# Batch 0 of a retention and mixer kernel: queries by head pairs in 1024-byte rows, scores of two units by head halves

## The chip, the cores and the metric

The kernel runs on one core of a Trainium2 chip. The metric is the device time of one execution in microseconds, as the median of several runs. Five engines run their own instruction streams and wait for each other by semaphores: TensorE (PE, with its weight loads shown as PEld), VectorE (DVE), ScalarE (ACT), GpSimd (POOL) and SyncE (SP, which here only issues DMAs).

## What is computed

```
q, k, v: [8, 8, 576, 64] float32           # batch, heads, positions, head size
scores = q @ k.T / 8                       # per batch and head
gamma  = 1 - 2 ** (-5 - head)
Dmat   = gamma ** (i - j) where i >= j, else 0
x      = (scores * Dmat) @ v               # [8, 576, 512], heads side by side
h      = x.T @ U @ V                       # U [576, 32], V [32, 576]: mixing along the positions
u      = x + h.T
out    = u + relu(u @ w1) @ w2             # w1 [512, 2048], w2 [2048, 512]
```

## The kernel before

The decay factorises: gamma^(i-j) = gamma^i * gamma^-j. So values are scaled by gamma^-j (`scale_u`, `scale_v`), the scores are only cut at the diagonal (`mask_u`), and the rows of the result are scaled by gamma^i (`XS_u`). Within a block of positions the scores are computed outright; what comes from earlier blocks goes through a running state k^T v (`ST_u`, copied to bf16 by `Sblk`) that the queries are multiplied with (`QS_u`). The MLP is the bulk of the work: `y1_items` holds the matmuls with w1 and the relu (L513, L518), `y2_items` those with w2 (L547).

The first two batches are handled apart from the rest. Each is cut in two *units* of 256 positions and one block of 64 (the "J" block). Batch 0 is units 0 and 1, batch 1 units 2 and 3. In a unit partition p holds positions 2p and 2p+1 of its 256, so that one DMA row has 2 x 64 values (512 bytes) of a head. `load_u(u, which)` issues on SP two DMAs of 256 KB, heads 0-3 and 4-7, for each of k, q and v asked for; they land in tiles of the `stage` pool (15 buffers). `cast_u` makes bf16 of such a tile (POOL, L613), `T_u` turns a whole tensor of a unit by sixteen transposes into one PSUM tile and copies it to SBUF (L628, then L639 on ScalarE or L641 on VectorE). For queries the copy also puts the even and odd positions back in order, so it writes every second element.

`SC_u(u, hh, ...)` computes the scores of four heads (hh 0: heads 0-3, hh 1: heads 4-7) by sixteen matmuls into a PSUM tile: `ps_sc` or `ps_o`, one buffer each, so the next scores in it wait for the mask that empties it. `mask_u` multiplies with the triangle on VectorE (L664). `RV_u` multiplies with the values.

The order on each engine is the order in the code (`manual_schedule`), and each engine takes its instructions in that order. `startup()` (from L812) holds the order up to the first MLP matmuls: first all loads on SP, then casts, turns, scores, masks and scalings. `warm(n)` issues n matmuls with no use for the result. SP gives each DMA one of eight semaphores in turn, so a DMA waits until the one eight places before it has landed. `load_w1(fb)` issues the DMA of a quarter of w1 (1 MB of float32, written as bf16) on POOL, between POOL's casts and scalings; there are four, and MLP columns f = 0-3, 4-7, ... need one each. `first_stretch()` (from L932) then mixes the MLP of batch 0 (`y(n)` issues the next n columns) with units 2 and 3; in each of these, TensorE turns keys and queries between MLP columns. From `main = ...` (L1073) on a merge of lists sets the order for the other batches.

Of the kernel before, what the change touches and what calls it, by code (L numbers as in the profile page):

```python
# [9 lines left out]
FP32 = mybir.dt.float32  # L10
BF16 = mybir.dt.bfloat16
# [25 lines left out]
def kernel(  # L37
# [11 lines left out]
    nc = tc.nc  # L49

    B, H, S, D = q.shape
    dm = H * D
    dff = moe_w_ch1.shape[1]
    R = moe_U.shape[1]
    P = 128
    HALF = 64
    NHP = H // 2
# [14 lines left out]
    stage = pool("stage", 15)  # L72
# [103 lines left out]
    def make_v():  # L176
        for c0, n in ((0, 4 * P), (4 * P, HALF)):
            ps = ps_big.tile([P, 4 * P], FP32, tag="big", name="pv")
            nc.tensor.matmul(
                ps[:, 0:n], fan.rearrange("k g r -> k (g r)"), V_b[:, c0:c0 + n],  # L180
                start=True, stop=True)
            nc.scalar.activation(
                out=V4[:, HALF + c0:HALF + c0 + n], in_=ps[:, 0:n], func=AF.Copy)

    def warm(n, pool_=None, tag="pss"):

        ps = (pool_ or ps_s).tile([P, 4, P], FP32, tag=tag, name="pw")
        for _ in range(n):
            nc.tensor.matmul(  # L189
                ps, ident, ident[:, None, :].to_broadcast([P, 4, P]), start=True, stop=True)  # L190
# [396 lines left out]
    def load_u(u, which):  # L587
        b = u // 2
        t0 = 2 * P * (u % 2) + HALF * b
        for j in which:  # L590
            dram = (q, k, v)[j]
            for hh in range(2):
                t = stage.tile([P, H, D], FP32, tag="stage", name="stage_t")
                un[u]["f", j, hh] = t
                nc.sync.dma_start(  # L595
                    out=t.rearrange("p (h j) d -> p h (j d)", j=2),
                    in_=dram[b, 4 * hh:4 * hh + 4, t0:t0 + 2 * P, :].rearrange(
                        "h (p j) d -> p h (j d)", j=2),
                )

    def unit_views(u, j, hh):
        if j not in un[u]:
            un[u][j] = qk_pool.tile([P, 2, dm], BF16, tag="qk", name="qk")
        w = slice(hh * 4 * D, (hh + 1) * 4 * D)
        return (un[u][j][:, :, w].rearrange("p j (h d) -> p h j d", d=D),
                un[u]["f", j, hh].rearrange("p (h j) d -> p h j d", j=2))
# [17 lines left out]
    def T_u(u, j, eng):  # L624
        pst = ps_big.tile([P, 2 * NHP, P], BF16, tag="big", name="pst")
        for jj in range(2):
            for hp in range(NHP):
                nc.tensor.transpose(  # L628
                    pst[:, jj * NHP + hp, :], un[u][j][:, jj, hp * P:(hp + 1) * P], ident)
        t = qkT_pool.tile([P, 2 * NHP, P], BF16, tag="qkT", name="qkT")  # L630
        un[u]["T", j] = t
        o, i_ = t, pst
        if j == 0:

            o = t.rearrange("p a b -> p (a b)").rearrange(
                "p (hp t j) -> p j hp t", hp=NHP, j=2)
            i_ = pst.rearrange("p (j hp) t -> p j hp t", j=2)
        if eng is nc.scalar:
            nc.scalar.activation(out=o, in_=i_, func=AF.Copy)  # L639
        else:  # L640
            eng.tensor_copy(out=o, in_=i_)  # L641

    def qT(u):
        return un[u]["T", 0].rearrange("p a b -> p (a b)").rearrange(
            "p (hp t) -> p hp t", hp=NHP)

    def SC_u(u, hh, pool_, tag):
        psc = pool_.tile([P, 2, NHP, P], FP32, tag=tag, name="psc")
        kT, qt = un[u]["T", 1], qT(u)
        for hp in range(2):  # L650
            for jj in range(2):
                for s in range(2):
                    for hl in range(2):
                        r = slice(hl * HALF, (hl + 1) * HALF)
                        m = slice(s * HALF, (s + 1) * HALF)
                        nc.tensor.matmul(  # L656
                            psc[m, hl, hp * 2 + jj, :], kT[r, jj * NHP + 2 * hh + hp, m],
                            qt[r, 2 * hh + hp, s * P:(s + 1) * P], start=True, stop=True,
                        )
        un[u]["psc", hh] = psc  # L660

# [30 lines left out]
    def QS_u(u, s, slot):  # L692
        for hp in range(NHP):
            nc.tensor.matmul(
                un[u]["po"][:, s, hp * P:(hp + 1) * P],
                qT(u)[:, hp, s * P:(s + 1) * P], sblk[:, slot, hp, :],
                start=False, stop=True, skip_group_check=True,
            )

# [107 lines left out]
    def cast_unit(u):  # L807
        for j in (1, 0):
            for hh in range(2):
                cast_u(u, j, hh, nc.gpsimd)  # L810

    def startup():  # L812
        load_u(0, (1, 0))
        load_v_rows()
        load_u(1, (1, 0))
        load_u(0, (2,))
        load_u(1, (2,))
        load(0, J, (1, 0, 2), seg=0)
        load_u_rows()
        load(0, J, (1, 0, 2), seg=1)  # L820
        load_u(2, (1, 0, 2))
        load_u(3, (1, 0, 2))
        nc.gpsimd.memset(st["x", 0][HI, J, :], 0.0)

        warm(10)
        cast_unit(0)
        T_u(0, 1, nc.vector)
        warm(5)
        nc.scalar.activation(out=V_b, in_=V_f, func=AF.Copy)
        T_u(0, 0, nc.scalar)  # L830
        make_v()
        warm(3)
        SC_u(0, 0, ps_sc, "psc")
        mask_u(0, 0)
        cast_unit(1)
        T_u(1, 1, nc.scalar)
        SC_u(0, 1, ps_o, "po")
        mask_u(0, 1)
        warm(2)
        T_u(1, 0, nc.scalar)  # L840
        scale_u(0, 0, nc.gpsimd)
        load_w1(0)
        scale_u(1, 0, nc.gpsimd)
        scale_u(1, 1, nc.gpsimd)
        cast_qk(0, J, LO, nc.gpsimd, js=(0,))
        scale_v(0, J, LO, nc.gpsimd)
        load_w1(1)
        cast_qk(0, J, HI, nc.gpsimd)
        scale_v(0, J, HI, nc.gpsimd)
        load_w1(2)  # L850
        scale_u(0, 1, nc.vector)
        warm(6)
        SC_u(1, 0, ps_sc, "psc")
        mask_u(1, 0)
        SC_u(1, 1, ps_o, "po")
        mask_u(1, 1)

        accA = pss_tile()
        accB = ps_big.tile([P, NHP, P], FP32, tag="big", name="pss2")
        ST_u(0, LO, accA, True)  # L860
        Sblk(accA, 0)
        ST_u(0, ALL, accB, True)
        Sblk(accB, 1)
        cast_qk(0, J, LO, nc.scalar, js=(1,))
        po_u(0, ps_sc, "psc")
        warm(2, ps_big, "big")
        RV_u(0, 0)
        RV_u(0, 1)
        QS_u(0, 1, 0)
        XS_u(0)  # L870
        warm(1, ps_big, "big")
        ST_u(1, LO, accB, False)
        Sblk(accB, 2)
        warm(1, ps_big, "big")
        RV_u(1, 0)
        RV_u(1, 1)
        T_J(LO, nc.vector)
        ST_u(1, HI, accB, False)
        Sblk(accB, 3)
        SC_J(LO)  # L880
        mask_J(LO)
        QS_u(1, 0, 1)
        QS_u(1, 1, 2)
        XS_u(1)
        make_ue()

        xT = [ps_big.tile([P, dm], FP32, tag="big", name="xT") for _ in range(3)]

        def to_xT(i, ccs):
            for cc in ccs:  # L890
                nc.tensor.matmul(
                    xT[cc][:, i * P:(i + 1) * P],
                    st["x", 0][:, i, cc * P:(cc + 1) * P], ident,
                    start=(i == 0), stop=True, skip_group_check=True,
                )

        for i in range(2):
            to_xT(i, range(3))
        RV_J(LO)
        QS_J(3)  # L900
        XS_J(LO)
        warm(2, ps_sc, "psc")
        xT.append(ps_sc.tile([P, dm], FP32, tag="psc", name="xT"))
        for i in range(2, J):
            to_xT(i, range(3))
        for i in range(J):
            to_xT(i, (3,))
        MA, _, _, _ = mixer_items(0, 0, split=True)
        MA((ps_o, "po"))
        warm(1)  # L910
        for cc in range(NCC):
            g = slice(cc * R, (cc + 1) * R)
            nc.tensor.matmul(
                xT[cc], st["a", 0][g, :], V4[g, HALF:HALF + 4 * P],
                start=False, stop=True, skip_group_check=True,
            )
        warm(1)
        for cc in range(NCC):
            o = st["uT", 0][:, :, cc, :]
            i_ = xT[cc].rearrange("p (s t) -> p s t", t=P)  # L920
            if cc % 2 == 0:
                nc.scalar.activation(out=o, in_=i_, func=AF.Copy)  # L922
            else:
                nc.vector.tensor_copy(out=o, in_=i_)
# [202 lines left out]
```

## Time and profile before

| | |
|---|---|
| median of 3 runs (lowest, highest) | 320.02 us (319.51, 321.42) |
| span of the profiled execution, first to last instruction | 318.7 us |
| the profiled execution's own time | not recorded apart from its span; the median run is 1.3 us longer than the span |
| busy: PE, DVE, ACT, POOL | 98%, 53%, 43%, 28% of the span |
| mean granted clock of TensorE | 1.00 |
| first MLP matmul (L513) | 23.73 us from the start |
| DMA share in 4 to 32 us | 1.0 to 1.3 of the core's 16 engines |

A profile line of the timeline reads: start, duration, engine, line, operation, output tile <- inputs, shape of output <- input, count, and in brackets the idle time of the engine before it with what ended it. The chain of waits lists start, duration and what the end of the program was waiting for at that time. A line of stages reads: from:to, length, then busy time (and number of instructions) of PE, PEld, DVE, ACT, POOL, then granted clock, DMA share, GB/s. A DMA share can pass 1, because packets of one DMA engine overlap.

### The profile page before, as it was taken

The page shows a single profiled execution, that of the slowest core. Times are in us where ns is not written, and L with a number is a line of the kernel's source. Part 1 is how long each engine was busy: PE and PEld are TensorE (multiplying, and loading weights), DVE is VectorE, ACT ScalarE, POOL GpSimd, SP SyncE. Part 2 cuts the span into 40 slices and gives each one's busy share as a digit, 9 for nine tenths or more (in the row PEclk, how much of TensorE's full clock was granted, in tenths as well). Part 3 has the DMA queues.
Part 4 walks back from the last instruction along what each step waited for, and adds up shares of the span by engine and source line. Part 5 has one row for each costly group of instructions (what it writes and reads, how often), then busy time and mean ns, then how long its engine had stood idle before and what let it go on. Part 6 is the DMA issues. An engine that isn't in the chain of part 4 may idle for free.

```text
span 318.7 us, 9166 instructions
## 1 busy us (share of the span) xinstructions
PE 311.4 (98%) x3929; PEld 167.7 (53%) x3929; DVE 169.1 (53%) x354; ACT 136.7 (43%) x293; POOL 90.3 (28%) x138
## 2 busy tenths in 40 slices
PE   8999899999999999999999999999999999999996
PEld 3564554554444444466644444466644444467544
DVE  5571466447995467545684468545674563500012
ACT  2757557772120465038720375048720463057400
POOL 5762933512232423132241423141241300110000
DMA  7999999999999979699994999598994710620022
GB/s 202 258 204 267 232 198 203 191 203 187 237 212 216 260 156 175 137 242 183 176 184 106 262 177 175 142 248 172 163 202 109 189 37 1 135 81 0 2 84 81
DMA packets 151321, 53.30 MB, mean 167 GB/s; under 512 B 131985, under 2 KB 148753, under 8 KB 151281
## 3 DMA queue, kind: packets, MB, share of 16 engines
q1 hardware_dynamic: 144512, 40.40, 70.2%
q0 software_dynamic: 6768, 12.32, 16.2%
q8 instruction: 30, 0.49, 0.7%
q14 instruction: 11, 0.08, 0.1%
HBM read 36.85 MB, written 9.44 MB: 145 GB/s over the span
## 4 chain that ended last, share of the span: by engine, by line
PE 84%; DMA 7%; ACT 3%; DVE 2%; issue 1%; SPq 1%; POOL 1%; ACTq 0%
PE ps_y L513 37%; PE ps_y L547 35%; DMA stage_t<-in_q_dram 5%; DMA qkT<-qk 2%; PE psc L279 2%; PE ph L454 1%; PE po L344 1%; PE ps_y L558 1%; PE po L361 1%; SPq L595 1%; PE psc L290 1%; PE pa L427 1%; ACT qkT L639 1%; PE psc L656 1%; PE pst L628 1%
## 5 line engine op out<-in xcount | busy, mean ns | idle before, releaser
L518 ACT ACTIVATE y<-ps_y 128x384 bf16<-128x384 f32 (+2 forms) x192 | 89.1, 489 | 105.1 <-PE ps_y L513 104.6
L513 PE MATMUL ps_y<-uT,w_sb 128*128 128x512 bf16 (+3 forms) x768 | 132.2, 326 | 0.7 <-ACT uT L922 0.4
L547 PE MATMUL ps_y<-w_sb,y 128*128 128x512 bf16 x560 | 126.3, 379 | 0.0
L513 PEld LDWEIGHTS <-w_sb 128*128 128x128 bf16 x768 | 70.2, 98 | 51.0 <-issue 2.4
L547 PEld LDWEIGHTS <-y 128*128 128x128 bf16 x560 | 52.7, 98 | 61.3
L536 DVE TENSOR_TENSOR o_sb<-ps_y,u 128x512 f32<-128x512 f32 (+2 forms) x38 | 25.2, 663 | 66.3 <-PE ps_y L547 63.9
L303 DVE TENSOR_TENSOR ret<-psc,tri 64x256 bf16<-64x256 f32 x108 | 45.3, 419 | 1.1
L539 POOL DMA_DIRECT2D out_dram<-o_sb x31 | 17.3, 558 | 98.6 <-DVE o_sb L536 95.7
L255 POOL TENSOR_TENSOR vt<-stage_t,vscale 128x512 bf16<-128x512 f32 (+1 forms) x29 | 30.2, 1041 | 52.3 <-DMA stage_t<-in_v_dram 44.6
L325 DVE TENSOR_TENSOR s_f<-psc,s_f 128x256 f32<-128x256 f32 x42 | 17.8, 423 | 26.2 <-PE psc L290 12.9
L460 DVE TENSOR_TENSOR u<-ph,xt 128x1024 bf16<-128x1024 f32 (+3 forms) x24 | 21.8, 951 | 9.3 <-PE ph L454 9.3
L246 ACT ACTIVATE qk<-stage_t 128x512 bf16<-128x512 f32 x27 | 16.9, 626 | 21.1 <-DMA stage_t<-in_q_dram 15.2
L372 DVE TENSOR_TENSOR xt<-po,qscale 128x512 bf16<-128x512 f32 x27 | 18.4, 681 | 1.8 <-PE po L344 1.8
L244 POOL CAST qk<-stage_t 128x512 bf16<-128x512 f32 x20 | 12.3, 614 | 23.6 <-DMA stage_t<-in_k_dram 21.4
L334 ACT ACTIVATE s_sb<-s_f 128x512 bf16<-128x512 f32 (+1 forms) x27 | 15.5, 575 | 3.8 <-DVE s_f L325 3.8
L315 DVE COPY vs<-vt 64x256 bf16<-64x256 bf16 x54 | 14.3, 265 | 1.2
L664 DVE TENSOR_TENSOR ret<-psc,triU 128x1024 bf16<-128x1024 f32 x8 | 9.6, 1222 | 9.2 <-PE psc L656 9.2
L189 PE MATMUL pw<-ident 128*128 128x512 bf16 x34 | 11.5, 461 | 1.4 <-POOL ident masks.py:199 1.4
L613 POOL CAST qk<-stage_t 128x512 bf16<-128x512 f32 x16 | 9.6, 613 | 9.9 <-DMA stage_t<-in_q_dram 5.3
L323 DVE COPY s_f<-psc 128x256 f32<-128x256 f32 x6 | 2.5, 424 | 16.4 <-PE psc L290 11.3
L279 PEld LDWEIGHTS <-qkT 64*64 64x64 bf16 x432 | 5.6, 107 | 9.6 <-issue 8.5
L433 ACT ACTIVATE a_sb<-pa 128x128 bf16<-128x128 f32 x8 | 2.2, 277 | 18.0 <-PE pa L427 18.0
(112 smaller groups left out, 191.4 us busy)
## 6 DMA issues: line engine op xcount, KB each, us to landing
stage_t<-in_k_dram SPq DMA_DIRECT2D x32, 256.0 KB, 4.8
stage_t<-in_q_dram SPq DMA_DIRECT2D x32, 256.0 KB, 5.3
stage_t<-in_v_dram SPq DMA_DIRECT2D x32, 256.0 KB, 5.5
out_dram<-o_sb POOLq DMA_DIRECT2D x31, 256.0 KB, 4.3
w_sb<-in_moe_w_ch_dram POOLq DMA_DIRECT2D x4, 512.0 KB, 8.0
w_sb<-in_moe_w_ch_dram POOLq DMA_DIRECT2D x8, 256.0 KB, 5.8
stage_t<-in_k_dram SPq DMA_DIRECT2D x8, 128.0 KB, 5.1
stage_t<-in_q_dram SPq DMA_DIRECT2D x8, 128.0 KB, 5.5
```

What stands on the lines that cost most here:

```text
L246: nc.scalar.activation(out=t[rows, 0, :], in_=c["f", 0][rows].rearrange("p h d -> p (h d)"), func=AF.Copy)
L255: (eng or nc.gpsimd).tensor_tensor(out=c["v"][rows], in0=c["f", 2][rows], in1=vscale[rows, i, :, None].to_broadcast([n, H, D]), op=ALU.mult,)
L303: nc.vector.tensor_tensor(out=ret[o, n], in0=c["psc"][t, hl, 0:SW].rearrange("p (hp i) -> p hp i", i=D), in1=tri[t, None, t].to_broadcast( ...
L325: nc.vector.tensor_tensor(out=f[:, t, :], in0=inc, in1=f[:, 1 - t, :], op=ALU.add)
L334: nc.scalar.activation(out=ch[pr, i]["s1"][:, w, :], in_=s_f[:, w, :], func=AF.Copy)
L372: nc.vector.tensor_tensor(out=xt[:, i, :].rearrange("p (hp hl d) -> p hl hp d", hl=2, d=D), in0=c["po"][:, :, 0:NHP * D].rearrange("p hl ( ...
L460: nc.vector.tensor_tensor(out=st["u", par][:, i0 - base:i0 - base + n, w].rearrange("p s (c d) -> p c s d", c=2), in0=ph[k][:, :, 0:n, :], ...
L513: nc.tensor.matmul(ps[:, 0:n, :], w1_sb[:, cc, f * P:(f + 1) * P], st["uT", par][:, c0:c0 + n, cc, :], start=(cc == 0), stop=(cc == NCC - 1),)
L518: nc.scalar.activation(out=st["y1", par][:, f, c0 * P:(c0 + n) * P], in_=ps[:, 0:n, :].rearrange("p s t -> p (s t)"), func=AF.Relu)
L536: nc.vector.tensor_tensor(out=o_sb[:, 0:n], in0=ps[:, 0:n], in1=st["u", par][:, c, w], op=ALU.add)
L539: (nc.sync if last else nc.gpsimd).dma_start(out=out_flat[r0:r0 + P, w], in_=o_sb[:, 0:n])
L547: nc.tensor.matmul(ps, st["y1", par][:, f, c * P:(c + 1) * P], w2_sb[:, f, :], start=(f == 0), stop=(f == NF - 1),)
```

## The change

Queries of batch 0 are no longer loaded by unit. `load_q4(hp)` loads two heads for both units at once: partition p holds positions 4p to 4p+3 of 512, a row is 4 x 64 values (1024 bytes), and there are four such loads of 256 KB, in the four places of the four query loads of before. `cast_q4` makes bf16 of one of them, `T_q4(g, engs)` turns two of them (four heads) by eight transposes and copies the result with one instruction per head pair, one on each engine named; the copy writes every fourth element. Then `qT_u` hands out the piece for a unit. Keys stay by unit; those of unit 1 are turned in two halves of four heads (`T_k`), each with four transposes and a copy of its own.

The order changes with it: scores and masks of heads 0-3 come for units 0 and 1 before those of heads 4-7. `scale_u(1, 0)` on POOL now stands ahead of the first `load_w1`. `warm(2)` goes and a `warm(6)` becomes `warm(3)`.

```diff
+    def load_q4(hp, eng=None):
+        t = stage.tile([P, H, D], FP32, tag="stage", name="stage_t")
+        q4["f", hp] = t
+        (eng or nc.sync).dma_start(
+            out=t.rearrange("p (h j) d -> p h (j d)", j=4),
+            in_=q[0, 2 * hp:2 * hp + 2, 0:4 * P, :].rearrange(
+                "h (p j) d -> p h (j d)", j=4),
+        )
+
+    def cast_q4(hp, eng):
+        g = hp // 2
+        if g not in q4:
+            q4[g] = qk_pool.tile([P, 2, dm], BF16, tag="qk", name="qk")
+        o = q4[g][:, hp % 2, :].rearrange("p (j h d) -> p h j d", j=4, d=D)
+        i_ = q4["f", hp].rearrange("p (h j) d -> p h j d", j=4)
+        copy(eng, o, i_)
+
+    def T_q4(g, engs):
+        pst = ps_big.tile([P, 2, 4, P], BF16, tag="big", name="pst")
+        for hp in range(2):
+            for j in range(4):
+                nc.tensor.transpose(
+                    pst[:, hp, j, :], q4[g][:, hp, j * P:(j + 1) * P], ident)
+        t = qkT_pool.tile([P, 2 * NHP, P], BF16, tag="qkT", name="qkT")
+        q4["T", g] = t.rearrange("p a b -> p (a b)").rearrange("p (hp t) -> p hp t", hp=2)
+        o = t.rearrange("p a b -> p (a b)").rearrange("p (hp t j) -> p hp j t", hp=2, j=4)
+        if engs[0] is engs[1]:
+            copy(engs[0], o, pst)
+        else:
+            for hp in range(2):
+                copy(engs[hp], o[:, hp], pst[:, hp])
...
+    def T_k(u, hh, eng):
+        if ("pst", 1) not in un[u]:
+            un[u]["pst", 1] = ps_big.tile([P, 2, NHP, P], BF16, tag="big", name="pst")
+            un[u]["T", 1] = qkT_pool.tile([P, 2 * NHP, P], BF16, tag="qkT", name="qkT")
+        pst = un[u]["pst", 1]
+        w = slice(2 * hh, 2 * hh + 2)
+        for jj in range(2):
+            for hp in (2 * hh, 2 * hh + 1):
+                nc.tensor.transpose(
+                    pst[:, jj, hp, :], un[u][1][:, jj, hp * P:(hp + 1) * P], ident)
+        copy(eng, un[u]["T", 1].rearrange("p (j hp) t -> p j hp t", j=2)[:, :, w, :],
+             pst[:, :, w, :])
+
+    def qT_u(u, hp, s):
+        if u < 2:
+            return q4["T", hp // 2][:, hp % 2, 2 * P * u + s * P:2 * P * u + (s + 1) * P]
+        return qT(u)[:, hp, s * P:(s + 1) * P]
...
     def startup():
-        load_u(0, (1, 0))
+        load_u(0, (1,))
+        load_q4(0)
+        load_q4(1)
         load_v_rows()
-        load_u(1, (1, 0))
+        load_u(1, (1,))
+        load_q4(2)
+        load_q4(3)
         load_u(0, (2,))
...
         warm(10)
-        cast_unit(0)
+        cast_u(0, 1, 0, nc.gpsimd)
+        cast_u(0, 1, 1, nc.gpsimd)
+        cast_q4(0, nc.gpsimd)
+        cast_q4(1, nc.gpsimd)
         T_u(0, 1, nc.vector)
         warm(5)
         nc.scalar.activation(out=V_b, in_=V_f, func=AF.Copy)
-        T_u(0, 0, nc.scalar)
+        T_q4(0, (nc.scalar, nc.vector))
         make_v()
+        cast_u(1, 1, 0, nc.gpsimd)
+        cast_u(1, 1, 1, nc.gpsimd)
+        cast_q4(2, nc.gpsimd)
+        cast_q4(3, nc.gpsimd)
         warm(3)
         SC_u(0, 0, ps_sc, "psc")
         mask_u(0, 0)
-        cast_unit(1)
-        T_u(1, 1, nc.scalar)
-        SC_u(0, 1, ps_o, "po")
-        mask_u(0, 1)
-        warm(2)
-        T_u(1, 0, nc.scalar)
+        T_k(1, 0, nc.scalar)
+        SC_u(1, 0, ps_o, "po")
+        mask_u(1, 0)
+        T_k(1, 1, nc.scalar)
+        T_q4(1, (nc.scalar, nc.vector))
         scale_u(0, 0, nc.gpsimd)
+        scale_u(1, 0, nc.gpsimd)
         load_w1(0)
-        scale_u(1, 0, nc.gpsimd)
         scale_u(1, 1, nc.gpsimd)
...
         scale_u(0, 1, nc.vector)
-        warm(6)
-        SC_u(1, 0, ps_sc, "psc")
-        mask_u(1, 0)
+        warm(3)
+        SC_u(0, 1, ps_sc, "psc")
+        mask_u(0, 1)
         SC_u(1, 1, ps_o, "po")
         mask_u(1, 1)
```

In `SC_u` and `QS_u` the queries `qT(u)[:, hp, ...]` become `qT_u(u, hp, s)`.

More of the change, by code (lines that the diff above doesn't have):

```diff
@@ L599, in load_u @@
                 )
+    def load_q4(hp, eng=None):
[27 more added lines that the diff above has]
+                copy(engs[hp], o[:, hp], pst[:, hp])
+    q4 = {}
     def unit_views(u, j, hh):
@@ L648, in SC_u @@
         psc = pool_.tile([P, 2, NHP, P], FP32, tag=tag, name="psc")
-        kT, qt = un[u]["T", 1], qT(u)
+        kT = un[u]["T", 1]
         for hp in range(2):
@@ L657, in SC_u @@
                             psc[m, hl, hp * 2 + jj, :], kT[r, jj * NHP + 2 * hh + hp, m],
-                            qt[r, 2 * hh + hp, s * P:(s + 1) * P], start=True, stop=True,
+                            qT_u(u, 2 * hh + hp, s)[r], start=True, stop=True,
                         )
@@ L695, in QS_u @@
                 un[u]["po"][:, s, hp * P:(hp + 1) * P],
-                qT(u)[:, hp, s * P:(s + 1) * P], sblk[:, slot, hp, :],
+                qT_u(u, hp, s), sblk[:, slot, hp, :],
                 start=False, stop=True, skip_group_check=True,
```

## The prediction

> **What bounds the kernel now.** I read the page first, then the stages, then the chain of waits, then the timeline of the first 40 us.
>
> ```profile
> span 318.7 us, 9166 instructions
> ...
> PE 311.4 (98%) x3929; PEld 167.7 (53%) x3929; DVE 169.1 (53%) x354; ACT 136.7 (43%) x293; POOL 90.3 (28%) x138
> ```
>
> TensorE is busy 98% of the span, but part of that is filler (`warm`, L189). So the stages count, cut at the first matmul of the MLP (L513, at 23.73 us) and at 48 us:
>
> ```profile
> 17.90:23.73 5.83, 5.26 (x111) 3.47 (x103) 3.50 (x7) 2.35 (x8) 4.09 (x6) 1.00 1.27 207
> ...
> 31.80:33.00 1.20, 0.11 (x2) 0.11 (x3) 0.60 (x1) 0.13 (x1) 0.61 (x1) 1.00 0.95 282
> 33.00:37.00 4.00, 4.00 (x64) 2.04 (x64) 1.22 (x1) 2.84 (x5) 3.79 (x5) 1.00 0.99 272
> ...
> 48.00:318.70 270.70, 267.30 (x3267) 142.68 (x3264) 144.39 (x309) 109.93 (x242) 61.78 (x87) 1.00 0.83 157
> ```
>
> The first two numbers are length and TensorE busy. Behind 23.73 TensorE has real work to the end. It idles 3.40 us after 48, where the change touches nothing, and 1.09 us in 31.8 to 33.0. An edit to the startup can change the total by no more than it moves the start of that work (23.73) and the waits in 23.73 to 48. The chain of waits names the large one:
>
> ```profile
> 20.87 11.30 DMA stage_t<-in_q_dram
> 32.17 0.05 issue
> 32.22 0.62 POOL qk L613
> ...
> 32.89 0.51 PE pst L628 x6
> ```
>
> The last query load of unit 2 is issued at 20.87 and lands at 32.17; its cast frees the transposes at 32.89. Before this, the startup's own chain:
>
> ```profile
> 8.70 1.31 ACT L639 ACTIVATE qkT<-pst 128x1024 bf16<-128x1024 bf16 x1 [0.17 <-PE pst L628]
> ...
> 11.07 1.02 ACT L639 ACTIVATE qkT<-pst 128x1024 bf16<-128x1024 bf16 x1 [0.49 <-PE pst L628]
> ...
> 12.54 1.32 ACT L639 ACTIVATE qkT<-pst 128x1024 bf16<-128x1024 bf16 x1 [0.45 <-PE pst L628]
> ...
> 13.15 0.75 DVE L617 TENSOR_TENSOR qk<-stage_t,vscaleU 128x512 bf16<-128x512 f32 x1 [0.27 <-DMA stage_t<-in_v_dram]
> ...
> 13.29 0.93 POOL L195 DMA_DIRECT2D w_sb<-in_moe_w_ch_dram  x1
> ...
> 14.37 2.36 DVE L664 TENSOR_TENSOR ret<-psc,triU 128x1024 bf16<-128x1024 f32 x2 [0.47 <-PE psc L656]
> ```
>
> Scores wait for ScalarE's turned queries, VectorE's masks (L664) for the scores, and from 14.37 VectorE is nearly full up to the last XS (21.68), so the pair of masks at 14.37 carries the start of the MLP.
>
> **Part 1, the query loads.** Still four DMAs of 256 KB on SP at the same four places, waiting for the same earlier landings; only the rows grow from 512 to 1024 bytes (512 rows per load become 256). In 6 to 13 us 4033 packets fill 113.9% of 16 engines: 7.0 x 16 x 1.139 / 4033 = 31.6 ns per packet. Of 1024-byte reads on this queue the trace has no row; the nearest are the 2048-byte output rows in 298 to 312 us, where 384 large packets (and 48 small ones) take 14.6%: 14 x 16 x 0.146 / 384 = 85 ns. A straight line through these two puts 1024 bytes at 49 ns, against 63 for two of 512. Casts follow their landings every 0.90 us (8.63, 9.51, 10.42, 11.32), so a load would take 0.90 x 49/63 = 0.70: 0.2 us less each, 0.8 for four. Bounds: nothing (bytes limit) and 0.45 each (packets limit), so 0 to 1.8. I take 0.8, since the rows differ in size as much as in direction. The DMA queues are full (share above 1.0 in all windows from 5.6 to 31.8), so what is saved moves every later landing.
>
> [...]
>
> **Part 2, turning and scores, first half.** The keys of unit 0 are as before. The eight transposes of T_q4(0) need both new casts (one by one 0.61 as before); the second ended at 8.09, with two loads' saving at 7.7. The copy is split: heads 0-1 on ScalarE, 2-3 on VectorE. But in the built program's order of instructions and waits VectorE's copy waits for ScalarE's. ScalarE's half: contiguous 128x512 takes 0.59; the spread rows cost 1.31 against 1.02 for 1024, so half of 0.29 more: 0.74. VectorE's half: between 0.43 (128x512, contiguous bf16, L724) and 0.69 (128x512 f32, L924); I take 0.69, a spread output. Together 0.74 + 0.05 + 0.69 = 1.48, against 1.31. ScalarE's V_b (L829, 7.84, 0.68) stands ahead, until 8.52, so the halves end at 9.26 and 10.0 at the latest, and the first sixteen scores end near 10.25 instead of 10.48: 0.2 us early. Its first mask then starts 0.2 early.
>
> **Part 3, second half.** Before, unit 1's keys and queries followed one another on ScalarE: 1.02, then 1.32, end 13.86. Now from 10.25: four transposes 0.3, copy 0.59, sixteen scores 0.4, four transposes 0.3 (near 11.95), copy 0.59 (12.6), ScalarE's queries 0.74 (13.35), VectorE's 0.69 (14.1). Casts are not the limit (the last ends at 11.93, now about 11.2). Then VectorE's queue matters: scale_u(0,1), 0.75, ran in the shadow of ScalarE's copy at 13.15. It is now queued behind VectorE's half, 14.1 to 14.85, and the two masks behind it start at 14.85 instead of 14.37: **0.48 late**. ST_u(0), which needs this scaling, is late by as much, and so are RV, XS and T_J. With 0.43 for VectorE's halves and overlap it would be 0.1 early; with no gain at the first scores 0.7 late. The other masks (heads 0-3 of unit 1) are hidden in 11.7 to 12.9, where VectorE waited.
>
> Five filler matmuls fewer (0.61 + 1.46 down to about 0.8 us): nothing, they stand in TensorE's waits; their cover gone is a rival below. Scores (4 x 16) and transposes (32) are as many as before.
>
> So the MLP starts at 23.73 + 0.48 = 24.2.
>
> **Part 4, w1 one scaling later.** On POOL the first w1 load (issue 13.29, 0.93) goes behind scale_u(1,0), 1.04, whose values land later than POOL is free: issue near 14.5, 1.2 late. It landed 7.7 after issue, at 21.0; now 22.2, and the MLP needs it at 23.0 or later: hidden by 0.8. The scaling of v of unit 1, second half, stays near 16.4, the later POOL work waits for landings (0.84 before L255, 1.53 before L724). The second w1 load runs behind the first in one queue. It landed at 19.09 + 8.3 = 27.4 and its matmuls started at 27.76: slack 0.4. They would now come at 28.2, and the load between 27.4 and 28.6: up to 0.4 of wait.
>
> In the time in which w1 has not started, SP's loads have the engines for themselves: 290 GB/s in 6 to 13, against 598 packets, 0.09 MB, in 15.5 to 18 when w1 runs. Unit 2's last queries landed just behind the third w1 load (23.58 + 8.8 = 32.4). With 0.8 saved and w1 1.2 late, SP's loads are ahead by 1 to 2 us of DMA time, so this load should slip in front of more of it.
>
> **Sum.** TensorE comes to the transposes at 31.8 + 0.48 = 32.3 and needs to wait only if the load is not there: before, it came 1.1 early. If the load comes at least 0.6 earlier, the matmuls run at 32.3 instead of 32.89: -0.6 us. If it comes as before, 0. I take the middle: **-0.3 us**. Behind it waits are small (0.24 us in 37 to 41, 0.04 in 41 to 48), on ScalarE's and VectorE's own work. The span of 318.7 becomes 318.4; the median of the runs, 320.02, lies 1.3 above that execution's span, so 319.7.
>
> **Rivals.**
> (a) *w1 too late* (slower). The second w1 load loses more than its issue, 2.0 us, landing at 29.4: its matmuls start 1.6 after 27.76, 1.1 of it is absorbed at unit 2's queries, so +0.5: 320.5. It decides from a landing past 28.9. For: slack of 0.4 only. Against: SP's loads are further by then.
> (b) *The clock* (slower). TensorE's filler takes 0.44 per matmul in the first 4.45 us (10 of them) and about 0.24 later (1.46 for six). Between 10.25 and 14.1 it is now busy for some 2.7 us of 3.85 (scores and transposes of part 3, 0.45 for T_q4's eight, 0.8 of filler), 70%; before, 3.73 of 4.10 (9.8 to 13.9), 91%. If that brings the slow rate back for four microseconds, the 4.0 busy us after 13.9 take up to twice their time; the masks and XS on VectorE hide more than half of that: +1.5, 321.5. Against: the granted clock reads 1.00 in every window, the first included.
> (c) *Rows of 1024 bytes land no earlier.* Only w1's delay helps the last queries; they come as before, the 0.48 is absorbed by the 1.1: 320.0.
> (d) *The halves are cheap*: both copies 0.4 to 0.5, masks on time or 0.1 early, load early: -1.1, 318.9.
>
> **How the numbers follow.** Forecast 0.45; (c) 0.22; (a) 0.17; (d) 0.08; (b) 0.08. The likeliest case alone spans 319.1 to 320.3; (d), less the 0.5 by which the fastest run of before lies under the median, takes the range to 318.4, (a) and (b) take it to 321.5. One per cent is 3.2 us, about what a measurement of this kernel can tell from no change. Only (b) with a longer slow stretch, or (a) repeated at the next w1 loads, reaches it upwards, 0.04; nothing in the 1.1 us to be had reaches it downwards, 0.02 for what I don't see.
>
> **What would show it.** Right: masks at 14.7 to 15.0, VectorE's query half behind ScalarE's, first L513 near 24.2, and the wait before the transposes of unit 2's queries (1.11) under 0.6. Wrong in the copies: the halves overlap, or masks at 14.4 or earlier. Wrong in the DMAs: casts still 0.90 apart at the queries, or the last query load of unit 2 still past 32. Wrong altogether: a changed idle time after 48 (3.40).

## The result, and the profile after

The changed kernel takes 324.63 us (median of 4 runs, 324.22 to 325.29), the kernel before 319.97 us (median of 4). The ratio is 1.0138, 95% interval 1.0112 to 1.0165: slower by 1.4%. The prediction said 319.7 us, at most 321.5. Its sign and its size are wrong.

The page of the changed kernel first:

```profile
span 322.8 us, 9155 instructions
...
PE 313.3 (97%) x3924; PEld 168.9 (52%) x3924; DVE 170.7 (53%) x356; ACT 136.6 (42%) x294; POOL 90.7 (28%) x138
...
PEclk9769999999999999999999999999999999999999
```

Shares of busy time have hardly moved. What is new is the last row, TensorE's granted clock in 40 slices of 8.07 us: the second and third slice read 0.7 and 0.6. The page of before has no such row, and its stages read 1.00. By stages (from:to, length, busy time of PE, PEld, DVE, ACT, POOL, clock, DMA share, GB/s):

```profile
8.10:11.50 3.40, 2.07 (x27) 0.95 (x25) 1.51 (x2) 1.84 (x3) 2.45 (x4) 1.00 1.14 314
8.40:11.80 3.40, 1.84 (x25) 0.84 (x23) 1.81 (x2) 1.87 (x4) 2.45 (x5) 0.97 1.15 309
11.50:12.00 0.50, 0.07 (x2) 0.00 (x0) 0.50 (x1) 0.40 (x1) 0.48 (x1) 0.57 1.18 292
...
13.90:17.90 4.00, 2.98 (x50) 1.73 (x50) 2.49 (x4) 1.48 (x2) 3.79 (x5) 0.50 1.20 158
...
31.80:33.00 1.20, 1.20 (x14) 0.54 (x12) 0.00 (x0) 0.93 (x3) 0.00 (x0) 1.00 1.15 332
...
48.00:322.80 274.80, 271.19 (x3328) 145.11 (x3326) 145.77 (x311) 110.81 (x244) 60.24 (x86) 1.00 0.81 153
```

Three things stand here. Between 11.5 and about 21.8 us the clock is at half; in the 3.4 us before its fall (8.1 to 11.5) TensorE was busy for 2.07. The wait of 1.09 us at 31.8 to 33.0 is gone (1.20 busy of 1.20): TensorE is now so late that it reaches unit 2's transposes only at 36.02. Behind 48 TensorE idles 3.61 us (274.80 - 271.19), against 3.40 before: nothing happens there. So the loss lies in the first 30 us. The chain of waits (start, length, what) shows what the startup now waits for:

```profile
8.23 1.32 ACT qkT L774
...
9.58 1.31 DVE qkT L776
...
10.93 0.31 PE psc L708 x8
...
14.33 1.32 ACT qkT L774
...
15.67 1.30 DVE qkT L776
...
28.06 0.59 ACT uT L984
...
28.69 1.11 PE ps_y L513 x4
```

And the timeline gives the tiles (in the brackets: idle time before, and what ended it):

```profile
8.23 1.31 ACT L774 ACTIVATE qkT<-pst 128x512 bf16<-128x512 bf16 x1 [0.19 <-PE pst L622]
...
9.58 1.30 DVE L776 COPY qkT<-pst 128x512 bf16<-128x512 bf16 x1 [3.05 <-ACT qkT L774]
...
15.67 1.29 DVE L776 COPY qkT<-pst 128x512 bf16<-128x512 bf16 x1 [1.50 <-ACT qkT L774]
16.77 0.71 DVE L651 TENSOR_TENSOR qk<-stage_t,vscaleU 128x512 bf16<-128x512 f32 x1
...
17.49 2.36 DVE L716 TENSOR_TENSOR ret<-psc,triU 128x1024 bf16<-128x1024 f32 x2
...
19.76 1.03 PE L737 MATMUL po<-qk,ret 64*128 64x64 bf16 x32
```

The same matmuls in the kernel before:

```profile
15.65 0.64 PE L685 MATMUL po<-qk,ret 64*128 64x64 bf16 x32
```

Each half of the queries' copy takes 1.3 us, as much as the whole copy of 1024 columns did before (1.31). The halves run one after the other, ScalarE first. The first masks begin at 11.28 instead of 10.53, and the pair of masks that carries the MLP begins at 17.49 instead of 14.37. The 32 matmuls of L737 take 1.03 us, where they took 0.64. The first MLP matmul comes at 28.69 instead of 23.73, 4.96 later; the span grows by 4.1.

### The profile page after: what moved, and what is told of

Its sections match the earlier page's. It is cut to its first block, busy times and chain, and to the rows that moved or that the text cites. A ratio compares the mean times of both kernels' runs of the same rounds, so it can differ in the third digit from the quotient of the medians.

```text
span 322.8 us, 9155 instructions
## 1 busy us (share of the span) xinstructions
PE 313.3 (97%) x3924; PEld 168.9 (52%) x3924; DVE 170.7 (53%) x356; ACT 136.6 (42%) x294; POOL 90.7 (28%) x138
## 4 chain that ended last, share of the span: by engine, by line
PE 87%; DMA 4%; DVE 3%; ACT 3%; issue 1%; SPq 0%; POOL 0%; ACTq 0%
PE ps_y L513 38%; PE ps_y L547 34%; DMA qkT<-qk 3%; PE psc L279 2%; DMA stage_t<-in_q_dram 1%; PE ph L454 1%; PE po L344 1%; PE ps_y L558 1%; PE pa L427 1%; ACT qkT L774 1%; PE po L361 1%; DVE qkT L776 1%; PE psc L708 1%; PE psc L290 1%; PE po L737 1%
## 5 line engine op out<-in xcount | busy, mean ns | idle before, releaser
L513 PE MATMUL ps_y<-uT,w_sb 128*128 128x512 bf16 (+3 forms) x768 | 132.4, 326 | 0.7 <-ACT uT L984 0.4
L513 PEld LDWEIGHTS <-w_sb 128*128 128x128 bf16 x768 | 70.2, 98 | 51.2 <-issue 2.7
L460 DVE TENSOR_TENSOR u<-ph,xt 128x1024 bf16<-128x1024 f32 (+3 forms) x24 | 21.8, 952 | 9.4 <-PE ph L454 9.4
L244 POOL CAST qk<-stage_t 128x512 bf16<-128x512 f32 x20 | 12.3, 614 | 23.4 <-DMA stage_t<-in_k_dram 18.2
L315 DVE COPY vs<-vt 64x256 bf16<-64x256 bf16 x54 | 13.1, 242 | 1.2
L344 PE MATMUL po<-vt,ret 64*64 64x64 bf16 x216 | 9.0, 193 | 0.0
```

The lines of the kernel that those rows point to most:

```text
L460: nc.vector.tensor_tensor(out=st["u", par][:, i0 - base:i0 - base + n, w].rearrange("p s (c d) -> p c s d", c=2), in0=ph[k][:, :, 0:n, :], ...
L513: nc.tensor.matmul(ps[:, 0:n, :], w1_sb[:, cc, f * P:(f + 1) * P], st["uT", par][:, c0:c0 + n, cc, :], start=(cc == 0), stop=(cc == NCC - 1),)
```

## The experiments

Ratios are against the kernel before, run beside it on the same chip.

**The copies by themselves.** A small kernel makes each kind of 128x512 copy twice, behind its transposes, with no scores, masks or MLP, and writes zeros as output. ScalarE's, VectorE's and GpSimd's copies run beside one another in it. Lines 54 to 60 are ScalarE from PSUM writing every element, every 2nd, 4th and 8th, L62 the same turn with the reads spread and the writes in sequence, L66 to L74 the same five on VectorE. Two of them:

```diff
+    nc.scalar.activation(out=ta.rearrange("p (t j) -> p j t", j=4), in_=pa, func=AF.Copy)                          # L58
+    nc.scalar.activation(out=ta.rearrange("p (t j) -> p t j", j=4), in_=pa.rearrange("p j t -> p t j"), func=AF.Copy)   # L62
```

> A kernel that holds only copies of 128x512, one at a time, beside a chip that does nothing else; it computes nothing of the reference and writes zeros. Theory S (the spacing of the written elements sets the price): bf16 copies take 0.59 us on ScalarE in sequence, 0.74 when every second element is written, 1.31 for every fourth, whether they read PSUM or SBUF; on VectorE 0.43, 0.6 to 0.7, 1.30. Written in sequence and read at a distance of 128 elements they take 0.6 and 0.4 to 0.7. Theory C (contention: the 1.31 in the changed kernel comes from transposes, DMA landings or the other engine at the same time): here every fourth element takes 0.74 or less on ScalarE and 0.69 or less on VectorE.

The groups of the small kernel, by shape (busy time of two, mean ns of one, idle before):

```profile
L60 ACT ACTIVATE ta<-pa 128x512 bf16<-128x512 bf16 x2 | 4.9, 2438 | 0.1
L72 DVE COPY td<-pd 128x512 bf16<-128x512 bf16 x2 | 4.8, 2424 | 0.1
...
L70 DVE COPY td<-pd 128x512 bf16<-128x512 bf16 x2 | 2.6, 1322 | 0.0
...
L58 ACT ACTIVATE ta<-pa 128x512 bf16<-128x512 bf16 x2 | 2.6, 1302 | 0.1
...
L56 ACT ACTIVATE ta<-pa 128x512 bf16<-128x512 bf16 x2 | 1.5, 740 | 0.1
L76 DVE COPY td<-b 128x512 bf16<-128x512 bf16 x2 | 1.5, 734 | 0.1
L68 DVE COPY td<-pd 128x512 bf16<-128x512 bf16 x2 | 1.4, 712 | 0.0
L74 DVE COPY td<-pd 128x512 bf16<-128x512 bf16 x2 | 1.4, 692 | 0.1
...
L54 ACT ACTIVATE ta<-pa 128x512 bf16<-128x512 bf16 x2 | 1.2, 597 | 7.0 <-PE pa L40 6.9
L62 ACT ACTIVATE ta<-pa 128x512 bf16<-128x512 bf16 x2 | 1.2, 597 | 0.1
L66 DVE COPY td<-pd 128x512 bf16<-128x512 bf16 x2 | 0.8, 424 | 5.1 <-PE pd L42 5.0
```

The price belongs to the spacing of what is written: 0.60, 0.74, 1.30 and 2.44 us on ScalarE for every element, every 2nd, 4th and 8th; 0.42, 0.71, 1.32 and 2.42 on VectorE. TensorE has nothing to do and no loads come in meanwhile, so contention with transposes and landings, as theory C had it, is out (the writes of the output run beside the copies). The other engine's copies do not set the price either: ScalarE's copies in sequence take 0.60 beside VectorE's cheapest (L54) and beside its dearest (L62). The same turn with the reads spread and the writes in sequence costs 0.60 and 0.69. One expectation missed: VectorE writing every 4th element from SBUF (L76) took 0.73, not about 1.3.

**Fewer fillers alone.** The kernel before with the change's edit of `warm` only:

```diff
-        warm(2)
...
-        warm(6)
+        warm(3)
```

> The kernel before, with the filler part of the change alone: warm(2) gone, warm(6) becomes warm(3). Theory W (the copies make TensorE wait, and the waits drop the clock): granted clock stays 1.00, first L513 within 0.2 us of 23.73, time within 0.5 us of before. Rival F (the five fillers themselves held the clock): clock 0.5 for several us after 13, first L513 at 25 or later, time up by 1.5 us or more.

Ratio 0.9999 (0.9969 to 1.0029), clock 1.00 in the profiled execution and 0.995 to 1.00 in the ten. The missing fillers alone cost nothing that this can tell. One expectation missed, the first L513 within 0.2 us of 23.73:

```profile
24.39 1.10 PE L513 MATMUL ps_y<-uT,w_sb 128*128 128x512 bf16 x4 [0.35 <-ACT uT L921]
...
29.36 0.62 POOL L613 CAST qk<-stage_t 128x512 bf16<-128x512 f32 x1 [0.23 <-DMA stage_t<-in_q_dram]
```

The masks are 0.23 early (14.14), but TensorE then stands still for 0.69 us ahead of 18.36, for nothing that the profile names. The second line matters more. It is unit 2's last query cast, at 32.22 in the trace of before. No load was touched here, and yet it comes 2.86 us earlier, and the wait of 1.1 us ahead of unit 2's transposes is not there. Where this load lands is thus not the same in every execution, and a single trace can't credit an edit with it.

**The changed kernel with TensorE kept busy.** Fillers in its waits: two between the halves of `T_q4(0)`, four inside the first scores, three behind `T_k(1, 0)`, and eight more at the second pair of halves.

```diff
+            if hp == 1 and g == 0:
+                warm(2)
...
-        SC_u(0, 0, ps_sc, "psc")
+        SC_u(0, 0, ps_sc, "psc", 4)
...
+        warm(3)
...
-        warm(3)
-        SC_u(0, 1, ps_sc, "psc")
+        warm(6)
+        SC_u(0, 1, ps_sc, "psc", 5)
```

> The kernel after, with fillers put into TensorE's waits (2 between the halves of T_q4(0), 4 inside the first scores, 3 before the second T_k half, 6 instead of 3 and 5 inside the scores of unit 0's second half): the copies are as they are. Theory W: the clock stays at 1.00, scores, transposes and RV run at their speed of before (32 RV matmuls 0.64 instead of 1.03), first L513 near 26.5 instead of 28.7, and of the 4.7 us lost some 2 come back: 322.6. Rival K (only the copies and the order count, the slow clock is hidden behind VectorE): first L513 stays at 28.4 or later, time 324 to 325.

```profile
8.40:11.80 3.40, 3.03 (x33) 1.37 (x31) 1.34 (x2) 1.85 (x3) 2.47 (x5) 1.00 1.15 310
11.80:15.20 3.40, 3.36 (x41) 1.76 (x40) 2.42 (x2) 2.28 (x3) 2.61 (x3) 1.00 1.32 206
```

Clock 1.00 throughout, ratio 1.0075 (1.0034 to 1.0116), first L513 at 26.84 instead of 28.69. Behind the masks, which stand at 17.47, the fallen clock was thus worth about 1.85 us. In the time it is 1.0138 - 1.0075 = 0.0063, 2.0 us, and by the two intervals, taken as independent, 0.4 to 3.6. 26.84 - 23.73 = 3.11 is what the late masks cost: 17.47 - 14.37 = 3.10. But the clock has a part in that lateness too. The masks did not move because the fillers delay the first pair of halves by 0.5 us and the scaling ahead of the masks (L653) takes 1.08 us instead of 0.71; from the first pair to the second it takes about 2.65 us here, against 3.45 at half clock.

**A PSUM tile for each half.** In the changed kernel the halves share a tile, and VectorE's waits for ScalarE's. With two tiles they run side by side:

```diff
-        pst = ps_big.tile([P, 2, 4, P], BF16, tag="big", name="pst")
+        pool2, tag2 = (ps_o, "po") if g == 0 else (ps_big, "big")
+        pst = [ps_big.tile([P, 4, P], BF16, tag="big", name="pst"),
+               pool2.tile([P, 4, P], BF16, tag=tag2, name="pst")]
```

> The kernel after, with a PSUM tile of its own for each half of T_q4, so that VectorE's copy no longer waits for ScalarE's. Theory W: both halves run at the same time, 1.3 us each, second scores and masks 1.3 earlier at each of the two places, masks of the second half at 15 or earlier instead of 17.5; with fewer waits the clock holds longer; first L513 at 25 to 26, time 321 to 322. Rival C (contention of the two engines in SBUF or PSUM): the overlapping halves take 2 us or more each and the masks move by less than 0.7.

```profile
8.22 1.33 ACT L776 ACTIVATE qkT<-pst 128x512 bf16<-128x512 bf16 x1 [0.23 <-PE pst L624]
8.44 1.31 DVE L778 COPY qkT<-pst 128x512 bf16<-128x512 bf16 x1 [1.03 <-PE pst L624]
...
14.90 2.34 DVE L718 TENSOR_TENSOR ret<-psc,triU 128x1024 bf16<-128x1024 f32 x2
```

Masks at 14.90, clock 1.00, first L513 at 24.26, ratio 1.0038 (1.0011 to 1.0065). Side by side each half still takes 1.3 us, so the halves do not slow one another. Most of the loss is back, some 0.4% stays. (Its profiled execution was its quickest, a span of 317.8, so that trace doesn't show the rest.)

**The changed kernel once more**, for a second trace of it:

> The changed kernel once more, for its clock: its four runs so far had mean granted clocks of 0.983, 0.984, 0.995 and 0.994 at times of 325.29 to 324.22. Theory W: a slow stretch again, begun where TensorE had been busy for about half of the 3.4 us before; by how long it lasts, first L513 lies between 26.8 and 28.7. Rival (the slow stretch of the first profile was a chance): granted clock 1.00 all along.

325.02 us, clock 0.989. There the clock is at half in two stretches, some 12.3 to 15.7 and 19.1 to 22.5 us, instead of in one. The first L513 comes at 29.09, past the 26.8 to 28.7 expected, because the masks begin at 18.30, behind a scaling that took 0.71 us in the first trace:

```profile
16.40 1.97 DVE L651 TENSOR_TENSOR qk<-stage_t,vscaleU 128x512 bf16<-128x512 f32 x1
```

GpSimd scales values at the same time; no run separates the cause. That the clock falls repeats, how long does not: the mean clock of the four earlier runs was 0.983, 0.984, 0.995 and 0.994, for 324.62, 325.29, 324.65 and 324.22 us. So its length alone doesn't set the time. All five executions of the changed kernel are at 0.995 or under; of the 78 of the kernel before that were run beside these experiments, six are.

**Copies in sequence.** Only the order in which T_q4's copy walks its elements is changed, to the cheap one of the small kernel; the halves stay serial:

```diff
-        o = t.rearrange("p a b -> p (a b)").rearrange("p (hp t j) -> p hp j t", hp=2, j=4)
+        o = t.rearrange("p a b -> p (a b)").rearrange("p (hp t j) -> p hp t j", hp=2, j=4)
+        pst = pst.rearrange("p hp j t -> p hp t j")
```

> The kernel after, with the turned queries written in sequence: the copy reads PSUM at a distance of 128 elements and writes every element in order, the same values to the same places. The halves still run one after the other. Theory S (the spacing of the written elements): 0.61 and 0.71 us instead of 1.31 and 1.30; masks of the second half near 14.6 instead of 17.5, the clock holds at 1.00, first L513 near 24.0, time 320 to 321 (ratio 0.999 to 1.003). Rival (the order and the rows lose by themselves): ratio stays above 1.007.

```profile
8.63 0.60 ACT L775 ACTIVATE qkT<-pst 128x512 bf16<-128x512 bf16 x1 [0.18 <-PE pst L622]
...
9.26 0.69 DVE L777 COPY qkT<-pst 128x512 bf16<-128x512 bf16 x1 [1.85 <-ACT qkT L775]
...
14.44 2.35 DVE L717 TENSOR_TENSOR ret<-psc,triU 128x1024 bf16<-128x1024 f32 x2
```

Ratio 1.0012 (0.9991 to 1.0034), masks at 14.44, first L513 at 24.45, clock 1.00 from 8.4 to 17.9 us (mean of its executions 0.994 to 1.00). Two lines give back 1.26 of the 1.38%, most of the clock's part included. The masks are where they were before (14.37), and still the MLP begins 0.72 late. Part of that is a wait of TensorE, 0.30 us at 17.45, for GpSimd's scaling of unit 1's second values, which starts at 16.33 here and was over at 16.32 before.

**Both together, and the same order in the kernel before.** First the two edits above in one kernel:

> The kernel after, written in sequence and with a PSUM tile for each half of T_q4, so the halves run at the same time. Theory S with W: both halves done 0.75 us after the transposes, masks of the second half at 13.8 to 14.2, first L513 at 23.2 to 23.6; TensorE's wait for unit 2's last queries (1.11 before) stays gone because the loads are 0.8 us ahead and w1 starts later, so the time falls by 0.5 to 1.3 us (ratio 0.996 to 0.9985). Rival D (what comes early at first L513 is given back at the next landing of w1 or of unit 2): ratio 0.999 to 1.002.

Masks at 13.59, 0.8 ahead of before, yet the ratio is 1.0018 (0.9990 to 1.0047): a miss. The MLP begins at 23.96; in this trace too TensorE waits for that scaling, 0.30 us at 16.60. In three of its twelve executions the mean clock is 0.989, with spans of 320.6 to 321.2 us; in the others it is 0.999 or 1.00, with 317.5 to 320.3. So the clock still falls in some executions, and these are longer by about 1.6 us (320.9 less 319.4, the means). Then T_u's query copy of the kernel before, written in sequence:

```diff
-                "p (hp t j) -> p j hp t", hp=NHP, j=2)
-            i_ = pst.rearrange("p (j hp) t -> p j hp t", j=2)
+                "p (hp t j) -> p hp t j", hp=NHP, j=2)
+            i_ = pst.rearrange("p (j hp) t -> p hp t j", j=2)
```

> The kernel before, with the copies of turned queries (T_u, four of them) written in sequence. Theory S: 1.02 us instead of 1.31 on ScalarE, first L513 0.3 to 0.5 earlier; unit 2's last queries land no earlier, so TensorE waits 0.3 to 0.5 longer for them and the time stays within 0.3 us (ratio 0.999 to 1.001). Rival (the start of the MLP sets the time): ratio 0.9985 or less.

Ratio 0.9992 (0.9972 to 1.0012); masks at 13.90, half a microsecond early, MLP at about 23.4. In both, the chain of waits no longer runs over the engines. It reads, for the second:

```profile
16.80 16.06 DMA stage_t<-in_v_dram x2
...
33.00 1.57 POOL qk L617 x2
...
35.03 8.21 DMA w_sb<-in_moe_w_ch_dram
```

Unit 2's values land at 32.86, 32.88 in the other trace; POOL scales them, then issues the last quarter of w1, and TensorE waits for it until 43.29, for 2.30 us (0.96 in the other). It does not wait for unit 2's last queries in this trace, against the expectation: their cast is at 30.59. In these two traces, with the copies cheap, the startup is bound by its loads. The clock stays at 1.00 around the long wait:

```profile
40.00:43.40 3.40, 1.10 (x20) 0.47 (x19) 1.23 (x1) 0.85 (x2) 2.40 (x4) 1.00 1.19 226
```

**w1 one scaling later, alone**, in the kernel before:

```diff
-        load_w1(0)
         scale_u(1, 0, nc.gpsimd)
+        load_w1(0)
```

> The kernel before with one edit only: the first load of w1 is issued behind the scaling of unit 1's values (scale_u(1,0)) instead of ahead of it. Theory H (hidden, the prediction's part 4): the landing moves from 21.0 to 22.2 at the latest, first L513 at 23.7 to 23.9, unit 2's last query load lands before 30, the wait of 1.11 us ahead of its transposes shrinks; ratio 0.997 to 1.001. Rival A (w1 too late): first L513 or the matmuls at 27.76 wait for w1; ratio 1.001 to 1.004.

```profile
35.12 1.04 PE L513 MATMUL ps_y<-uT,w_sb 128*128 128x512 bf16 x4 [1.67 <-DMA w_sb<-in_moe_w_ch_dram]
...
43.80 1.04 PE L513 MATMUL ps_y<-uT,w_sb 128*128 128x512 bf16 x4 [0.36 <-DMA w_sb<-in_moe_w_ch_dram]
```

Ratio 1.0007 (0.9982 to 1.0033), the first L513 at 23.97. Unit 2's last query cast comes at 30.35 instead of 32.22 (30 was expected at the latest) and the wait ahead of its transposes is gone. But the wait is also missing in two traces in which no load was moved (casts at 29.36 with fewer fillers, 30.59 with copies in sequence), so theory H is not shown by it. In this trace TensorE waits 1.67 us for the third quarter of w1, which rival A did not name either: it had put the wait at the first or second.

**The last quarter of w1 ahead of the scaling of unit 2's values**, in the two kernels with copies in sequence:

```diff
-            if last:
-                load_w1(u)
...
+            if not last:
+                load_w1(3)
             scale_u(u, 0, nc.gpsimd)
```

> The kernel before with the query copy of T_u written in sequence, and the last quarter of w1 issued on POOL ahead of the scaling of unit 2's values instead of behind it. With the copy alone the chain of waits ended in unit 2's values landing at 32.9, their scaling on POOL, the issue of this load at 35.0 and its landing at 43.2. Theory: the load is issued at 31.2 to 32.8, lands by 41 to 42 and TensorE doesn't wait for it; ratio 0.994 to 0.998, a version faster than both. Rival D (the DMA engines are full until then, whatever the order): the load takes the time from unit 2's values or lands at 43 again; ratio 0.998 to 1.002.

Ratio 1.0064 (1.0031 to 1.0098).

> The changed kernel with copies in sequence, a PSUM tile for each half, and the last quarter of w1 ahead of the scaling of unit 2's values. TensorE waited 0.96 us for this quarter at 43.2 before this edit. Theory: that wait goes; ratio to the kernel before 0.997 to 1.000. Rival D (DMA engines full): it stays between 0.5 and 1.0 us, or moves to unit 2's scaled values; ratio 1.000 to 1.003.

Ratio 1.0052 (1.0025 to 1.0078). TensorE's wait for that quarter is gone in both, and both are slower, by their medians beyond either theory. In the first, unit 3's last two casts move from about 37.0 to 38.23, after a wait of 2.60 us for its queries; in the second the scaling of unit 3's values begins at 42.31 instead of 38.21, after 3.99 us of waiting; and at 93 us TensorE waits 0.87 and 1.11 us for turned keys that were there in time without the edit. The loads that the quarter has overtaken are late in these two traces; how much of that is the edit's doing one trace each can't tell. These waits do not add up to the whole half per cent. No version here beats the kernel before beyond its interval.

## Why the prediction was wrong

**The step that failed** is the price of T_q4's copies in parts 2 and 3: 0.74 + 0.69 us a pair, measured 1.31 + 1.30. I took half of the surcharge of the old copy (0.29 us for 1024 columns). But the old copy wrote every second element and the new one every fourth. By the small kernel 512 columns cost 0.14 us more at spacing 2, and 0.70 more at spacing 4. The nearest row was not of the same kind, and the upper bound I gave (0.69 for VectorE) was a bound for writing in sequence. For an honest upper end there was no row at all.

From there the masks' lateness adds up in the trace of the changed kernel. The first pair of halves ends at 10.88, not 10.0: 0.88. From there to the second pair it takes 3.45 us, not 2.6, on a TensorE at half clock: 0.85. The second pair lasts 2.63, not 1.5: 1.13. Together 2.86; the masks came 2.64 after the 14.85 forecast, as the scaling between them began a little ahead of the copy's recorded end. The order of events was right throughout: VectorE's half behind ScalarE's, the scaling of unit 0's second values (L651) behind that half, the masks behind the scaling.

**The second failure is rival (b), the clock**, with 0.08 and +1.5 us. It happened, with the dear copies one behind the other in all five executions and with cheap ones in few, and cost about 2 us (0.4 to 3.6). I had put TensorE at 70% between 10.25 and 14.1 with cheap copies, and argued against the rival from a clock of 1.00 everywhere. For 70% the trace of before had a row (2.29 busy of 3.40 us in 29.6 to 33.0, 67%, at 1.00). With the dear copies TensorE was busy for 61% before the fall (2.07 of 3.40; 1.40 in the second trace, 8.9 to 12.3), no 3.4 us of that trace's startup were as low, and the clock went to 0.50.

The two failures explain the size. Of the 4.96 us at the first MLP matmul 0.48 was forecast. The copies add 0.88 + 1.13 = 2.01. The clock goes with 1.85 behind the masks and with most of the 0.85 between the pairs, which at full clock, with the fillers, is almost gone (2.65 against the 2.6 forecast): together about 2.65. The scaling takes 0.22 off. The spans differ by 4.1 only: the trace of before held the wait of 1.1 us for unit 2's queries, and TensorE is now too late to meet it. Neither rival of the prediction combined the two, and the range ended at 321.5.

**Part 1 was right in sign, and in size by luck.** The values behind the four query loads reach their scaling on POOL at 11.52 in the changed kernel instead of 12.29 before, 0.77 us early where 0.8 was forecast:

```profile
12.29 1.06 POOL L617 TENSOR_TENSOR qk<-stage_t,vscaleU 128x512 bf16<-128x512 f32 x1 [0.36 <-DMA stage_t<-in_v_dram]
...
11.52 1.06 POOL L651 TENSOR_TENSOR qk<-stage_t,vscaleU 128x512 bf16<-128x512 f32 x1 [0.40 <-DMA stage_t<-in_v_dram]
```

But these two are the latest and the earliest of their kind. The five traces with the old loads have 11.64 to 12.29, the seven with the new ones 11.52 to 11.92; their means differ by 0.38 us. Steadier is the time from unit 1's second key cast to this scaling, with two query loads in between: 2.76 to 2.80 us with the old rows, 2.52 to 2.65 with the new. That is about 0.12 us a load, not 0.2. Rival (c), by which the longer rows land no earlier, is out by that little.

**Part 4 saw the wait go, but the runs don't show that its mechanism did it.** The first w1 load was issued at 14.31 (1.0 late, 1.2 forecast) and landed at 20.2, in time. Unit 2's last query cast came at 28.87 instead of 32.22. But this landing moves by itself: the cast is at 28.65 to 32.22 in the four traces in which neither these loads nor the first w1 load were edited, and at 28.73 to 32.56 in the seven with the change. And with transposes at 36.02, the 32.22 of before would have been early enough. The gain of 0.3 us in the sum thus rested on one execution's wait. In the trace of the same move alone TensorE waits 1.67 us at the third quarter of w1, a quarter that part 4 did not follow; here the MLP was 5 us late and would have hidden it. **Fewer fillers at no cost** was right for the kernel before; in the changed one, seventeen more in the waits kept the clock at 1.00 in all five executions.

What stays open: what in TensorE's waits brings the clock down, and how long it stays there, since two executions of one kernel differ; why the scaling ahead of the masks takes from 0.68 to 1.97 us; and whether the 0.4% that a tile for each half does not give back is more than copies in sequence leave (0.1%), since the two intervals overlap.

## What to carry to other kernels

When a turn or a regrouping is folded into a copy, let the copy write in sequence and put the spacing on the side that is read from PSUM: here this halves the price (1.30 to 0.60 us on ScalarE, 1.32 to 0.69 on VectorE), and it cost two lines. Price a strided copy only from a row with the same spacing, and where there is none, take the spacing as a multiplier for the upper end (here spacing 2, 4 and 8 cost 1.2, 2.2 and 4.1 times the copy in sequence on ScalarE, 1.7, 3.1 and 5.7 times on VectorE). Waits of about a microsecond on TensorE in a startup can cost twice, once as a wait and once as a slower clock behind it: here they did at 11 us (a wait of 1.03 us, then a clock of 0.50), while one of 2.30 us at 41 us did not (1.00). A load that is pulled forward while the DMA queues are full may gain nothing: in the windows of 8 us behind the last quarter of w1 (28 to 36 us, 32 to 40 us) the DMA share was 0.96 to 1.20, other loads were late in these two traces, and the ratios were 1.0064 and 1.0052. And before a wait for a load becomes a term of a sum, look at a second execution for it.

## What the runs showed of the hardware

- Copies of 128x512 bf16 out of PSUM cost 0.60, 0.74, 1.30 and 2.44 us on ScalarE for spacing 1, 2, 4 and 8 of the written elements, and 0.42, 0.71, 1.32 and 2.42 on VectorE; reading PSUM 128 elements apart costs ScalarE nothing (0.60) and VectorE 0.27. From SBUF, VectorE writes every 4th element in 0.73, while ScalarE (1.34) and GpSimd (1.32, against 0.62 in sequence) pay in full. Why the spacing costs time is not shown.
- The granted clock fell to 0.50 at 11.5 us in the changed kernel: in 8.1 to 11.5 us TensorE's longest wait was of 1.03 us, its busy share 61% (2.07 of 3.40). It stayed down for some 10.2 us there, and for 3.4 us twice in the second trace. The busy share alone does not decide: the clock stayed at 1.00 with a tile for each half through 1.92 busy of 3.40 us (56%, line below), and in the kernel before with copies in sequence through 1.10 of 3.40 (32%), around a wait of 2.30 us. By which rule it falls is not shown.

```profile
10.40:13.80 3.40, 1.92 (x36) 1.28 (x39) 3.19 (x3) 2.39 (x3) 2.14 (x4) 1.00 1.23 262
```
